# A new hand-made order for attention and two expert layers on one core: other priorities, more filler matmuls, and three edits to the loads

## The chip, the cores and the metric

The kernel runs on 1 core of one Trainium2 chip. Its time is device microseconds (us) of one execution. The kernel before has a median of 481.8 us over 3 runs (479.96 to 482.65).

## The reference

q, k and v have the shape (2, 8, 576, 64): 2 batches, 8 heads, 576 positions of 64 elements. Two attentions are added, and their sum passes through two expert layers (names and checks cut):

```python
q_d, k_d, v_d = (x.reshape(B, H, S // 4, 4, D).mean(axis=3) for x in (q, k, v))
out_up = np.repeat(softmax(scale * q_d @ k_d.T) @ v_d, 4, axis=2)   # 144 positions
mask = abs(pos[:, None] - pos[None, :]) < 4                         # band of 7
out_local = softmax(where(mask, scale * q @ k.T, -1e9)) @ v
x = (out_up + out_local)            # reshaped to 1152 tokens x 512
h = x @ w_in                        # 512 x 2048, float64 in memory
P = a[0] + a[1] * h + a[2] * h**2 + a[3] * h**3
Q = 1.0 + abs(b[0]) * abs(h) + abs(b[1]) * h**2
x = (P / (Q + 1e-06)) @ w_out       # 2048 x 512
h = x @ w_in2
out = (h * tanh(softplus(h))) @ w_out2
```

## The kernel before, in words

The attention is cut into 18 units. A unit is 256 query rows: four windows of 64 positions for a pair of heads, or, for the last 64 positions of a batch, one window for each of the four pairs (the two "mixed" units). For a unit TensorE (PE) transposes the queries (line 552), adds the mask and computes the banded scores (712, 720) and the coarse scores (728), transposes the softmax (797, 802) and multiplies with v (827, 837). In between VectorE (DVE), ScalarE (ACT) and GpSimd (POOL) do the maxima, exponentials, normalisation and copies. Each pair of heads of a batch needs its keys first (lines 552 on PE, 593 on ACT, 603 on DVE). The sum goes as high and low halves into `xh` and `xl`.

The first layer multiplies `xh` and `xl` with `w_in` (line 1155) in three products that give float32 accuracy, applies the rational function, and multiplies with `w_out` (line 1288); its first columns start while attention still runs. The second layer is at lines 1469, 1525 and 1290, with sums of blocks (1329, 1491). Weights come as float64: a load of 1 MB (994, 999), two passes on ACT (1011, 1018), one or two on DVE (1025, 1031), and a split in halves (1037, 1042).

All loads are issued by SyncE (SP) in one queue, with at most 8 under way. The constants `a` and `b` are two small loads from SP (483, 484); ACT takes absolute values of them (515, 516) and DVE derives six numbers (`leading`, 520 to 525).

The order of everything is written out beforehand. Each step is a task with a priority (a due time), engines it may run on with assumed costs, and buffers. `Plan.run` steps through an assumed time and gives every free engine the ready task of the smallest priority. Each engine then executes its instructions in this order and waits on semaphores where data are late. Priorities come from tables: `UOFF` shifts the 18 units, `GOFF` the first weights, `LEAD`, `CLEAD`, `LLEAD`, `OLAG` and `SUMS` whole kinds of tasks.

A filler matmul on zeros (`warm`, line 533, 128x480 in bf16) is counted wherever the assumed time leaves PE idle and a PSUM bank is free. It is emitted only in the window `SHOW`, from 2.4 to 30 us of the assumed time:

```python
if SHOW[0] <= now < SHOW[1]:
    shown = fns[-1](s.view)
```

Of the kernel before, what the change touches and what calls it, by code (L numbers as in the profile page):

```python
# [23 lines left out]
EDGE, LEAST = 2.0 ** -60, 1e-30  # L24


SECOND = 1.8
COLD, FILL_ALL = 3.4, 20
WINDOW, FILL, FILL_END = 3.4, 0.9, 450.0
SHOW = (2.4, 30.0)  # L30
LEAD, CLEAD, LLEAD, OLAG = 38, 14, 40, 18
PROL, PSTEP, VOFF, VROFF, LOFF, KOFF = -45, 2.5, 2, -1, 7, 9
GROUPS = ([6, 6, 4], [4, 4, 4, 4])
KCUT, MIX = 4, (1, 4)
MKP = -45
NKN, NVW, NXT, NQN = 2, 2, 3, 3
XVR, XQN, XVW = 2, 0, 0
SUMS = 5
NRAW, NWT, NRING, NRING2 = 2, 2, 3, (2, 1)
LAT = {"pe": 0.2, "act": 0.16, "dve": 0.15, "pool": 0.15, "sp": 1.1}  # L40
QUEUED = 8
UOFF = [-3.0, 0.0, 0.0, 3.0, 4.5, 3.0, 3.0, -1.5, 6.0, 0.0, 0.0, -4.5, -4.5, 4.5, 6.0, 4.5, -1.5, -1.5]
GOFF = [0.0, 0.0, 0.0, 0.0, -4.0, -4.0, -10.0, -6.0, 2.0, -4.0, 10.0, 12.0]
HP = 15


# [4 lines left out]
def t_dve(n, fast=False, ptr=0):  # L51
    return 0.068 + n * (0.000521 if fast else 0.001042) + 0.06 * ptr
# [28 lines left out]
class Plan:  # L81
# [33 lines left out]
    def run(self, names):  # L115
# [80 lines left out]
        while True:  # L196
            for e in names:
                if until[e] > now:
                    continue
                held = []  # L200
                while ready[e]:
                    item = heapq.heappop(ready[e])
                    t = item[2]
                    if t.started:
                        continue
                    one = next(iter(t.engs))
                    if e != one and until[one] + t.engs[one] <= now + t.engs[e] + SECOND:
# [12 lines left out]
                    end = until[e] = begin + t.engs[e] * (2 if e == "pe" and now < COLD else 1)  # L220
                    there = end + LAT[e]
                    if t.dma:
                        end = begin
                        for issue, move in t.dma:
                            end = max(end, landed[-QUEUED]) + issue
                            moved = max(moved, end + 0.3) + move
                            landed.append(moved + LAT["sp"])
                        until[e], there = end, landed[-1]
                    n += 1
                    heapq.heappush(events, (end, n, 0, e, t))  # L230
                    heapq.heappush(events, (there, n, 1, e, t))
# [43 lines left out]
def kernel(  # L275
# [13 lines left out]
    nc = tc.nc  # L289
    B, H, S, D = q.shape  # L290
# [7 lines left out]
    TW = 384  # L298
# [68 lines left out]
    kn_s = lay("att", NKN, 768, parts=96)  # L367
    vr_s = lay("att", 1, 1024, (4, 4, D), parts=72)
    qn_s = lay("att", NQN, 256)
    vw_s = lay("att", NVW, 512, (4, 2, D), parts=64 + WK)  # L370
    s_s = lay("att", 2, 256, (4, 64))
    pd_s = lay("att", 2, SD)
# [107 lines left out]
        nc.gpsimd.memset(bias1[:, 1:2], 1e-06)  # L480

    def c_sp():
        nc.sync.dma_start(out=a_sb, in_=a.partition_broadcast(128))
        nc.sync.dma_start(out=b_sb, in_=b.partition_broadcast(128))

    add({"act": 1.3}, lambda: nc.scalar.preload_act_table_set("natural_log_exp_and_others"), -1000)
    t_id = add({"pool": 1.1}, lambda: make_identity(nc, ident), -1000)
    t_m = add({"dve": 0.1}, lambda: nc.vector.memset(band, 0.0), -1900)
    t_cd = add({"dve": 0.6}, zeros, -1000)
    add({"dve": 0.4}, lambda: None, -880)  # L490
    t_bn = add({"pool": 0.5}, bands, -900, after=[t_m])
    def mask_set(lo, hi, ws):
        for w in ws:
            masks(*w)
# [2 lines left out]
    t_mk = [  # L497
        add({"dve": cost}, lambda x=x: mask_set(*x), pr, after=[t_bn])
        for cost, pr, x in (
            (0.4, -890, (0, 4, ((0, 0, 1), (0, 1, 1), (0, 2, 1), (0, 3, 1)))), (0.25, MKP, (3, 7, ((1, 4, 4),))),  # L500
            (0.25, MKP, (7, 11, ((2, 8, 4),))),
        )
    ]
    t_bias = add({"pool": 0.1}, biases, -20)
    t_i16 = add({"dve": 0.26}, eyes, -900, after=[t_id])
    t_ab = add({"sp": 0.9}, c_sp, -34, dma=[(0.65, 0.1), (0.5, 0.1)])
    A0, A1, A2, A3 = (cf[:, i:i + 1] for i in range(4))
    S0, S1 = (cf[:, i:i + 1] for i in range(4, 6))

# [16 lines left out]
        tiny(cf[:, 0:3], a_sb[:, 0:3], S0, ALU.mult)  # L526

    t_b = add({"act": 0.25}, absolute, -30, after=[t_ab])
    t_b = add({"dve": 0.6}, leading, -30, after=[t_b])


    def warm(view):
# [21 lines left out]
    def prep(bb, p, prio, slots, start):  # L554
# [58 lines left out]
            dst = vr.v.rearrange("p (h t) f d -> p h (t f d)", h=2)  # L613
            nc.sync.dma_start(out=dst, in_=src)

        m0 = add({"sp": 1.25}, vload, prio + VROFF, take=[vr], chain="vr", dma=[(0.65, 0.8), (0.6, 0.12)])

        def va(e):
            tv = vr.v
# [14 lines left out]
    def unit(u, slots, start):  # L634
# [1 line left out]
        pairs = sorted({p for p, _ in wins})  # L636
        mixed = len(pairs) > 1
        xq, xv = (wide_s["qn"], wide_s["vw"]) if start else ([], [])
        qn, vw, qp, qT, qx = Buf(qn_s + xq), Buf(vw_s + xv), Buf(slots["q"]), Buf(qT_s), Buf(qx_s)
        sc, pt, po, px = Buf(slots["s"]), Buf(slots["pt"]), Buf(slots["po"]), Buf(px_s)  # L640
        tm, s, pd, pT, od, xt = Buf(tm_s), Buf(s_s), Buf(pd_s), Buf(pT_s), Buf(od_s), Buf(xt_s)
        mix = [qx] if mixed else []

        def qload():
            for i, p in enumerate(pairs):
                w, m = wins[i][1], n // len(pairs)
                src = q[bb, 2 * p:2 * p + 2, 64 * w:64 * w + 2 * m, :]
                nc.sync.dma_start(
                    out=qn.v[m * i:m * i + m].rearrange("p (r h d) -> p r h d", h=2, d=D),
                    in_=src.rearrange("h (p r) d -> p r h d", r=2),  # L650
                )

        l0 = add({"sp": 0.65}, qload, prio - LOFF, take=[qn], chain="ld", dma=[(0.65, 0.24)] * 4 if mixed else [(0.65, 0.58)])

        m0 = MASK0[kind]
        keys = [(p, [window(kind, w, b) for b in range(2)]) for p, w in wins]
# [10 lines left out]
                        in_=bass.AP(src.tensor, src.offset + k0 * D, [[D, WK], [far * D, 4], [1, D]]),  # L667
                    )

        vl = add({"sp": 1.0}, vload, prio + VOFF, take=[vw], chain="vw", dma=[(0.45, 0.11)] * 8 if mixed else [(0.45, 0.33)] * 4)  # L670

        def pe_a():
            q2 = qp.v[:, :2 * n].rearrange("c (p r) -> c p r", r=2)
            for r in range(2):
                flip(q2[:, :, r], qn.v, r, n)
# [30 lines left out]
        def pe_b():  # L706
# [24 lines left out]
                        )  # L731

        tb = add(
            {"pe": 1.6 if mixed else 0.86}, pe_b, prio,
            after=tq + [kv_done[p] for p in pairs] + [t_i16, t_mk[kind]],
            take=[sc, tm, s, pd],
            use=[qT] + mix, chain="pb",
# [707 lines left out]
    def seven(st):  # L1445
# [42 lines left out]
        def plus(dst, i, src, after, and_=None):  # L1488
            def fn():
                other = two(dst)[:, i]  # L1490
                nc.vector.tensor_tensor(out=other, in0=src.v[:, :TW], in1=other, op=ALU.add)

            return add({"dve": t_dve(TW)}, fn, pr, after=after, use=[src, dst])

        p1 = prod(A, cols(0, 0), x1[:2], 0, 0, 0, [], [A])
        k1 = copy(low, 0, A, [p1], [low])
# [88 lines left out]
```

## Time and profile before

| | |
|---|---|
| median of 3 runs | 481.8 us |
| profiled execution | 481.31 us |
| its span | 479.5 us |
| PE busy | 467.6 us (98%) |
| DVE, ACT, POOL busy | 376.8, 337.6, 58.7 us |
| granted TensorE clock over the span | 0.993 |

The span leaves 1.8 us of the profiled execution outside. A matmul's row ends when its last column has left the array, so rows of matmuls that follow each other overlap; how densely PE works is read from the starts. Idle time before a row stands in brackets with what ended it. A granted clock of 1.00 is 2.4 GHz, 0.5 is 1.2 GHz.

### The profile page before, as it was taken

The numbers are of one execution on the slowest core, as the hardware profiler recorded it, in microseconds if no ns is written. First come the engines' busy times: TensorE is split into PE (matmuls) and PEld (weight loads), VectorE is DVE, ScalarE is ACT, GpSimd is POOL, SyncE is SP. The second block draws the span as 40 slices with busy tenths as digits, with TensorE's granted clock in tenths as the row PEclk, the third lists the DMA queues.
The fourth block names the chain that finished last, engine by engine and source line by source line (L and its number), as shares of the span: only waits on it lengthen the run. The fifth ranks groups of instructions, "written<-read, shape, count | busy, mean of one in ns | idle before, by whom it ended". The sixth has DMA issues, their size and how long they took to land.

```text
span 479.5 us, 9855 instructions
## 1 busy us (share of the span) xinstructions
PE 467.6 (98%) x4081; PEld 428.5 (89%) x4081; DVE 376.8 (79%) x566; ACT 337.6 (70%) x529; POOL 58.7 (12%) x80
## 2 busy tenths in 40 slices
PE   8999898999999999999999999999999999999996
PEld 4667797889999999999999998898989898989885
DVE  6688789899899978997999989988596669524342
ACT  5778698885988799998878797578667446422320
POOL 2654345653000000000000000000000000000000
PEclk9999799999999999999999999999999999999999
DMA  8967976611422402333022022134314220000103
GB/s 180 234 172 176 263 184 182 153 42 36 168 89 90 143 34 87 106 130 117 0 89 89 1 89 87 45 115 143 137 21 156 87 89 0 1 0 2 66 1 131
DMA packets 45757, 47.17 MB, mean 98 GB/s; under 512 B 30352, under 2 KB 31120, under 8 KB 45712
## 3 DMA queue, kind: packets, MB, share of 16 engines
q1 hardware_dynamic: 45712, 46.54, 33.4%
q8 instruction: 32, 0.52, 0.5%
q14 instruction: 13, 0.11, 0.1%
HBM read 44.17 MB, written 2.36 MB: 97 GB/s over the span
## 4 chain that ended last, share of the span: by engine, by line
PE 74%; DVE 12%; DMA 8%; ACT 3%; issue 1%; SPq 1%; ACTq 0%
PE psum L1290 19%; PE psum L1155 18%; PE psum L1288 15%; PE psum L1469 11%; PE psum L1525 5%; DMA att<-in_q_dram 3%; DMA raw<-in_moe_w_in_dram 3%; PE psum L837 1%; DMA att<-in_v_dram 1%; PE psum L827 1%; DVE wt L1025 1%; PE psum L552 1%; DVE xl L1311 1%; DVE wrk L1329 1%; PE psum L728 1%
## 5 line engine op out<-in xcount | busy, mean ns | idle before, releaser
L1155 PE MATMUL psum<-xh,wi 128*128 128x384 f32 (+1 forms) x336 | 84.7, 323 | 0.2 <-DVE wrk L1184 0.2
L1288 PE MATMUL psum<-gg,wo 128*128 128x384 f32 (+1 forms) x480 | 76.2, 313 | 0.0
L1288 PEld LDWEIGHTS psum<-gg,wo 128*128 128x128 f32 x480 | 72.8, 189 | 0.5 <-issue 0.2
L1155 PEld LDWEIGHTS psum<-xh,wi 128*128 128x128 f32 x336 | 60.2, 193 | 1.5 <-issue 0.9
L1155 PE MATMUL psum<-xl,wi 128*128 128x384 f32 (+1 forms) x168 | 53.1, 316 | 0.0
L1290 PE MATMUL psum<-wo,gg 128*128 128x512 f32 x216 | 51.7, 391 | 0.0
L1290 PE MATMUL psum<-wo,late_g 128*128 128x512 f32 x216 | 51.3, 391 | 0.0
L1290 PEld LDWEIGHTS psum<-wo,late_g 128*128 128x128 f32 x216 | 40.4, 188 | 8.0
L1290 PEld LDWEIGHTS psum<-wo,gg 128*128 128x128 f32 x216 | 40.4, 188 | 8.0
L1025 DVE SCALAR_TENSOR_TENSOR wt<-wt,raw 128x1024 int32<-128x1024 int32 x32 | 40.4, 1266 | 7.5 <-ACT wt L1011 6.5
L1011 ACT ACTIVATE wt<-raw 128x1024 f32<-128x1024 f32 x32 | 36.4, 1137 | 8.7 <-DVE wo L1042 4.8
L1018 ACT ACTIVATE raw<-raw 128x1024 int32<-128x1024 uint16 x32 | 36.8, 1149 | 4.7 <-DMA raw<-in_moe_w_out_dram 3.4
L1525 PE MATMUL psum<-xh,wi 128*128 128x384 f32 x128 | 34.5, 335 | 0.0
L1155 PEld LDWEIGHTS psum<-xl,wi 128*128 128x128 f32 x168 | 32.5, 193 | 0.0
L1401 DVE TENSOR_TENSOR part<-psum,part 128x512 f32<-128x512 f32 x27 | 17.8, 687 | 13.6 <-PE psum L1290 13.6
L1155 PE MATMUL psum<-xh,late_r 128*128 128x384 f32 x96 | 25.5, 334 | 0.0
L1175 ACT ACTIVATE wrk<-psum 128x768 f32<-128x768 f32 (+1 forms) x27 | 19.9, 735 | 6.6 <-PE psum L1155 6.0
L1037 ACT ACTIVATE wo<-wt 128x1024 fp32r<-128x1024 f32 x11 | 11.7, 1061 | 17.7 <-DVE wt L1031 7.7
L1042 DVE TENSOR_TENSOR wo<-wt,wo 128x1024 fp32r<-128x1024 f32 x14 | 17.1, 1218 | 8.7 <-ACT wo L1037 8.7
L1525 PEld LDWEIGHTS psum<-xh,wi 128*128 128x128 f32 x128 | 23.3, 188 | 0.2
L1099 ACT ACT_TABLE_LOAD x17 | 21.8, 1283 | 0.3
L1525 PE MATMUL psum<-xl,wi 128*128 128x384 f32 x64 | 21.4, 335 | 0.0
(164 smaller groups left out, 1038.5 us busy)
## 6 DMA issues: line engine op xcount, KB each, us to landing
raw<-in_moe_w_in_dram SPq DMA_DIRECT2D x16, 1024.0 KB, 5.4
raw<-in_moe_w_out_dram SPq DMA_DIRECT2D x16, 1024.0 KB, 4.9
att<-in_v_dram SPq DMA_DIRECT2D x72, 48.0 KB, 4.0
out_dram<-part SPq DMA_DIRECT2D x9, 256.0 KB, 2.0
att<-in_q_dram SPq DMA_DIRECT2D x16, 128.0 KB, 3.9
att<-in_k_dram SPq DMA_DIRECT2D x6, 288.0 KB, 3.8
att<-in_v_dram SPq DMA_DIRECT2D x6, 288.0 KB
wrk<-in_k_dram SPq DMA_DIRECT2D x2, 288.0 KB, 6.2
```

The source lines that it names most:

```text
L1011: nc.scalar.activation(out=t.v, in_=words(r)[:, :, 1].bitcast(F32), func=AF.Prelu if fold else AF.Identity, scale=2.0 ** -112, **({"alpha" ...
L1018: nc.scalar.activation(out=words(r)[:, :, 0], in_=r.v.bitcast(U16).rearrange("p (n four) -> p n four", four=4)[:, :, 1], func=AF.Copy, sca ...
L1025: nc.vector.scalar_tensor_tensor(out=ti, in0=ti, scalar=3, in1=words(r)[:, :, 0], op0=ALU.logical_shift_left, op1=ALU.bitwise_or)
L1042: ENG[e].tensor_tensor(out=w.v[:, 1], in0=s.v, in1=w.v[:, 0].bitcast(F32), op=ALU.subtract)
L1099: nc.scalar.preload_act_table_set(name)
L1155: nc.tensor.matmul(st.h.v[:, i, :T], w.v[:, ww, ks], xx[:, kk, c0:c0 + T], start=(nn == 0 and (st.big or i == 0)), stop=(nn == 3 * KD - 1 ...
L1175: nc.scalar.activation(out=vw(st.a), in_=H(), func=AF.Square)
L1288: nc.tensor.matmul(A(d)[:, :T], w.v[:, ww, lo + d * 128:lo + (d + 1) * 128], vw(gg)[:, i, :], start=start, stop=stop)
L1290: nc.tensor.matmul(A(d), vw(gg)[:, i, sl], w.v[:, ww, lo:lo + DM], start=start, stop=stop)
L1401: nc.vector.tensor_tensor(out=pv, in0=acc.v[:, j], in1=pv, op=ALU.add)
L1469: nc.tensor.matmul(dst.v[:, :TW], wv.v[:, ww, at:at + 128], x(h, kk), start=bool(take) and nn == 0, stop=nn == 5, skip_group_check=not take,)
L1525: nc.tensor.matmul(h.v[:, i, :TW], w.v[:, ww, at:at + 128], xx[:, kk, c0:c0 + TW], start=nn == 0, stop=nn == 3 * KD - 1)
```

## The change

The tables and constants of the order are new (of `UOFF` and `GOFF` the first lines only). `SHOW` now ends at 450 us, so nearly all counted fillers are emitted. The assumed time of a DMA grows by 0.8 us for every 7.0 us of transfer (`FETCH`). The two loads of constants are issued by ACT, ahead of its first table load; `leading` is computed inside the softmax step of the third unit. A mixed unit loads its queries in one DMA of 64 x 8 x 64 into two neighbouring query buffers and transposes them with four matmuls, instead of four DMAs and two matmuls. The second layer's additions (`plus`) get an earlier due time.

```diff
-SECOND = 1.8
+SECOND = 1.6
-SHOW = (2.4, 30.0)
-LEAD, CLEAD, LLEAD, OLAG = 38, 14, 40, 18
-PROL, PSTEP, VOFF, VROFF, LOFF, KOFF = -45, 2.5, 2, -1, 7, 9
+LEAD, CLEAD, LLEAD, OLAG = 38, 20, 30, 22
+PROL, PSTEP, VOFF, VROFF, LOFF, KOFF = -45, 2.5, 2, 2, 5, 9
-SUMS = 5
+SUMS = 20
-UOFF = [-3.0, 0.0, 0.0, 3.0, 4.5, 3.0, 3.0, -1.5, 6.0, 0.0, 0.0, -4.5, -4.5, 4.5, 6.0, 4.5, -1.5, -1.5]
+FETCH = (0.8, 7.0)
+SHOW = (2.4, 450.0)
+UOFF = [1.5, 0.0, 1.5, 12.0, 13.5, 13.5, 9.0, 18.0, 12.0, 9.0, -3.0, -6.0, -1.5, -3.0, 7.5, 10.5, -1.5, -9.0]
...
-                            moved = max(moved, end + 0.3) + move
+                            first = max(moved, end + 0.3)
+                            moved = first + move + FETCH[0] * (int((first + move) / FETCH[1]) - int(first / FETCH[1]))
...
+    qm_s = [Place("att", qn_s[-2].lo, 512, (8, D), 64)]
...
     def c_sp():
-        nc.sync.dma_start(out=a_sb, in_=a.partition_broadcast(128))
-        nc.sync.dma_start(out=b_sb, in_=b.partition_broadcast(128))
+        nc.scalar.dma_start(out=a_sb, in_=a.partition_broadcast(128))
+        nc.scalar.dma_start(out=b_sb, in_=b.partition_broadcast(128))
...
-    t_ab = add({"sp": 0.9}, c_sp, -34, dma=[(0.65, 0.1), (0.5, 0.1)])
+    t_ab = add({"act": 1.15}, c_sp, -2000, dma=[(0.65, 0.1), (0.5, 0.1)])
...
-    t_b = add({"dve": 0.6}, leading, -30, after=[t_b])
+    t_b = add({"dve": 0.6}, lambda: None, -30, after=[t_b])
...
         def qload():
-            for i, p in enumerate(pairs):
...
+            if mixed:
+                nc.sync.dma_start(out=qn.v, in_=q[bb, :, 64 * w:64 * w + 64].rearrange("h s d -> s h d"))
...
         def pe_a():
+            if mixed:
+                for i in range(nw):
+                    nc.tensor.transpose(
+                        qp.v[:, 64 * i:64 * i + 64], qn.v[:, 2 * i:2 * i + 2].rearrange("s h d -> s (h d)"), ident[:64, :64],
+                    )
+                return
...
             nc.vector.reciprocal(out=tm.v[:, 10:15], in_=tm.v[:, 10:15])
+            if (bb, kind, pairs[0]) == (0, 0, 2):
+                leading()
...
-            return add({"dve": t_dve(TW)}, fn, pr, after=after, use=[src, dst])
+            return add({"dve": t_dve(TW)}, fn, pr - HP, after=after, use=[src, dst])
```

Of instructions, PE has 111 fillers instead of 61, 80 transposes of keys and queries instead of 84 and 8 smaller ones; SP has 10 loads fewer and 2 of a new kind; ACT has the 2 loads of constants and 30 conversions of weights instead of 29, DVE 2 instead of 3 (line 1039). Everything else is the same work in another order.

The first place is ACT's start. Before, in the kernel's own line numbers:

```order
L486 ACT_TABLE_LOAD
L593 ACTIVATE att<-psum 64x288 x4
L682 ACTIVATE att<-psum 128x256
L593 ACTIVATE att<-psum 64x288 x4
L682 ACTIVATE att<-psum 128x256
```

Now (the copies of keys are at line 595):

```order
L486 DMA a_sb<-in_moe_a_dram 128x4
L487 DMA b_sb<-in_moe_b_dram 128x2
L489 ACT_TABLE_LOAD
L517 ACTIVATE b_sb<-b_sb 128x2
L518 ACTIVATE cf<-a_sb 128x4
L595 ACTIVATE att<-psum 64x288 x4
L691 ACTIVATE att<-psum 128x256
```

The two loads and the two absolute values, which need them landed, stand ahead of the first copies of keys.

The second place is SP's queue around the constants and the first mixed unit's queries, before:

```order
L994 DMA raw_75<-in_moe_w_in_dram 128x4x256
L483 DMA a_sb<-in_moe_a_dram 128x4
L484 DMA b_sb<-in_moe_b_dram 128x2
L665 DMA att<-in_v_dram 48x4x64 x8
L994 DMA raw_74<-in_moe_w_in_dram 128x4x256
L648 DMA att<-in_q_dram 32x4x64 x4
L564 DMA att<-in_k_dram 96x12x64
```

And now:

```order
L668 DMA att<-in_v_dram 48x4x64 x8
L651 DMA att<-in_q_dram 128x4x64
L1005 DMA raw_75<-in_moe_w_in_dram 128x4x256
L651 DMA att<-in_q_dram 128x4x64
L668 DMA att<-in_v_dram 48x4x64 x4
L1005 DMA raw_74<-in_moe_w_in_dram 128x4x256
L616 DMA att<-in_v_dram 72x2x512
L668 DMA att<-in_v_dram 48x4x64 x4
L649 DMA att<-in_q_dram 64x8x64
L566 DMA att<-in_k_dram 96x12x64
```

The constants are gone from it, and one load stands for the four of the mixed unit.

The third place is PE at the first mixed unit's product with v, before:

```order
L728 MATMUL psum<-att 32x144 x4
L797 MATMUL psum<-ident,att 112x128 x2
L802 MATMUL psum<-ident,att 72x128 x2
L827 MATMUL psum<-att 64x16 x16
L837 MATMUL psum<-att 64x32 x16
L552 MATMUL psum<-ident,att 128x96 x3
```

And now:

```order
L535 LDWEIGHTS blank
L535 MATMUL psum<-blank 128x480
L808 MATMUL psum<-ident,att 112x128 x2
L813 MATMUL psum<-ident,att 72x128 x2
L535 LDWEIGHTS blank
L535 MATMUL psum<-blank 128x480
L838 MATMUL psum<-att 64x16 x16
L848 MATMUL psum<-att 64x32 x16
L554 MATMUL psum<-ident,att 128x96 x3
```

Fillers (line 535) now stand on both sides of the transposes of the softmax: three ahead, of which the last is shown, and one behind. Over the whole order 71 fillers stand before the first matmul of the first layer (61 before), 39 in the rest of the attention (none before) and 1 later.

## Rows read from the trace of the kernel before

**Rows 1.** The page's busy times: share of the span, instructions.

```profile
PE 467.6 (98%) x4081; PEld 428.5 (89%) x4081; DVE 376.8 (79%) x566; ACT 337.6 (70%) x529; POOL 58.7 (12%) x80
```

**Rows 2.** Stretches: length, busy PE, PEld, DVE, ACT, POOL; clock, DMA share, GB/s.

```profile
0.00:120.00 120.00, 112.89 (x2144) 92.10 (x2144) 101.30 (x244) 91.67 (x227) 57.98 (x79) 0.97 0.68 162
120.00:260.00 140.00, 140.00 (x846) 140.00 (x844) 127.36 (x140) 123.61 (x144) 0.75 (x1) 1.00 0.28 98
```

**Rows 3.** PE in order of time, fillers: start, duration, line [idle before].

```profile
9.42 1.58 PE L533 MATMUL psum<-blank 128*128 128x480 bf16 x7
10.84 0.41 PE L552 MATMUL psum<-ident,wrk 96*128 96x96 f32 x3
```

**Rows 4.** PE in order of time, waits before 31 us.

```profile
7.34 0.69 PE L552 MATMUL psum<-ident,att 96*128 96x96 f32 x6 [0.47 <-DMA att<-in_k_dram]
9.14 0.44 PE L552 MATMUL psum<-ident,att 128*128 128x128 f32 x2 [0.34 <-DMA att<-in_q_dram]
```

**Rows 5.** PE in order of time, waits from 31 to 120 us.

```profile
35.60 0.28 PE L1155 MATMUL psum<-xl,wi 128*128 128x256 f32 x1
35.72 0.28 PE L1155 MATMUL psum<-xh,wi 128*128 128x256 f32 x1
36.41 0.45 PE L827 MATMUL psum<-att 72*64 72x64 f32 x8 [0.42 <-DVE att L857]
...
39.94 0.41 PE L552 MATMUL psum<-ident,att 128*128 128x128 f32 x2 [0.51 <-DMA att<-in_q_dram]
...
50.71 0.30 PE L837 MATMUL psum<-att 48*64 48x32 f32 x2
52.51 1.03 PE L837 MATMUL psum<-att 48*64 48x32 f32 x30 [1.50 <-DMA att<-in_v_dram]
...
76.57 0.69 PE L552 MATMUL psum<-ident,att 96*128 96x96 f32 x5 [1.13 <-ACT att L593]
77.99 0.40 PE L797 MATMUL psum<-ident,att 128*112 128x128 f32 x2 [0.72 <-POOL att L786]
...
99.69 0.38 PE L1155 MATMUL psum<-xh,wi 128*128 128x256 f32 x1 [0.20 <-DVE wrk L1184]
```

**Rows 6.** Stretches around the lower clock, columns as in Rows 2.

```profile
52.00:56.00 4.00, 3.49 (x63) 3.21 (x67) 2.39 (x4) 1.98 (x5) 1.83 (x4) 0.57 1.03 377
56.00:60.00 4.00, 4.00 (x49) 3.50 (x42) 2.76 (x6) 1.77 (x6) 0.38 (x1) 0.57 0.97 127
```

**Rows 7.** PE's waits: total us, times, longest.

```profile
PE psum L1469 <- DVE wrk L1491: 0.9, 1, 0.9
```

**Rows 8.** SP's queue in order of time: start, duration until issued.

```profile
23.74 1.65 SPq L483 DMA_DIRECT2D a_sb<-in_moe_a_dram  x1
25.43 1.17 SPq L484 DMA_DIRECT2D b_sb<-in_moe_b_dram  x1
26.65 6.19 SPq L665 DMA_DIRECT2D att<-in_v_dram  x8
...
33.38 2.62 SPq L648 DMA_DIRECT2D att<-in_q_dram  x4
```

**Rows 9.** The page's DMA issues: count, KB each, median us to landing.

```profile
out_dram<-part SPq DMA_DIRECT2D x9, 256.0 KB, 2.0
...
att<-in_k_dram SPq DMA_DIRECT2D x6, 288.0 KB, 3.8
...
a_sb<-in_moe_a_dram SPq DMA_DIRECT2D x1, 2.0 KB, 8.0
b_sb<-in_moe_b_dram SPq DMA_DIRECT2D x1, 1.0 KB, 6.5
```

**Rows 10.** ACT in order of time, its start and the absolute values.

```profile
0.73 1.28 ACT L486 ACT_TABLE_LOAD   x1 [0.73 <-PEq L1569]
5.00 1.75 ACT L593 ACTIVATE att<-psum 64x288 f32<-64x288 f32 x4 [2.99 <-PE psum L552]
...
32.56 0.19 ACT L515 ACTIVATE b_sb<-b_sb 128x2 f32<-128x2 f32 x1
```

**Rows 11.** DVE in order of time, first and last of seven instructions of `leading`.

```profile
32.87 0.16 DVE L520 TENSOR_REDUCE cf<-cf 128x1 f32<-128x4 f32 x1 [0.73 <-ACT cf L516]
...
33.90 0.23 DVE L512 TENSOR_SCALAR cf<-a_sb,cf 128x3 f32<-128x3 f32 x1
```

More of the change, by code (lines that the diff above doesn't have):

```diff
@@ L41 @@
 QUEUED = 8
-UOFF = [-3.0, 0.0, 0.0, 3.0, 4.5, 3.0, 3.0, -1.5, 6.0, 0.0, 0.0, -4.5, -4.5, 4.5, 6.0, 4.5, -1.5, -1.5]
-GOFF = [0.0, 0.0, 0.0, 0.0, -4.0, -4.0, -10.0, -6.0, 2.0, -4.0, 10.0, 12.0]
+FETCH = (0.8, 7.0)
+SHOW = (2.4, 450.0)
+UOFF = [1.5, 0.0, 1.5, 12.0, 13.5, 13.5, 9.0, 18.0, 12.0, 9.0, -3.0, -6.0, -1.5, -3.0, 7.5, 10.5, -1.5, -9.0]
+GOFF = [0.0, 2.0, 0.0, 2.0, -4.0, -4.0, -4.0, -20.0, 18.0, 0.0, -6.0, 22.0]
 HP = 15
@@ L489 @@
     t_cd = add({"dve": 0.6}, zeros, -1000)
-    add({"dve": 0.4}, lambda: None, -880)
-    t_bn = add({"pool": 0.5}, bands, -900, after=[t_m])
+    t_bn = add({"pool": 1.0}, bands, -900, after=[t_m])
     def mask_set(lo, hi, ws):
@@ L499 @@
         for cost, pr, x in (
-            (0.4, -890, (0, 4, ((0, 0, 1), (0, 1, 1), (0, 2, 1), (0, 3, 1)))), (0.25, MKP, (3, 7, ((1, 4, 4),))),
-            (0.25, MKP, (7, 11, ((2, 8, 4),))),
+            (0.8, -890, (0, 4, ((0, 0, 1), (0, 1, 1), (0, 2, 1), (0, 3, 1)))), (0.5, MKP, (3, 7, ((1, 4, 4),))),
+            (0.5, MKP, (7, 11, ((2, 8, 4),))),
         )
@@ L614, in vload @@
             nc.sync.dma_start(out=dst, in_=src)
-        m0 = add({"sp": 1.25}, vload, prio + VROFF, take=[vr], chain="vr", dma=[(0.65, 0.8), (0.6, 0.12)])
+        m0 = add({"sp": 0.65}, vload, prio + VROFF, take=[vr], chain="vr", dma=[(0.65, 1.0)])
         def va(e):
@@ L638, in unit @@
         xq, xv = (wide_s["qn"], wide_s["vw"]) if start else ([], [])
-        qn, vw, qp, qT, qx = Buf(qn_s + xq), Buf(vw_s + xv), Buf(slots["q"]), Buf(qT_s), Buf(qx_s)
+        qn, vw, qp, qT, qx = Buf(qm_s if mixed else qn_s + xq), Buf(vw_s + xv), Buf(slots["q"]), Buf(qT_s), Buf(qx_s)
         sc, pt, po, px = Buf(slots["s"]), Buf(slots["pt"]), Buf(slots["po"]), Buf(px_s)
@@ L644, in qload @@
         def qload():
-            for i, p in enumerate(pairs):
-                w, m = wins[i][1], n // len(pairs)
-                src = q[bb, 2 * p:2 * p + 2, 64 * w:64 * w + 2 * m, :]
+            w = wins[0][1]
+            if mixed:
+                nc.sync.dma_start(out=qn.v, in_=q[bb, :, 64 * w:64 * w + 64].rearrange("h s d -> s h d"))
+            else:
                 nc.sync.dma_start(
-                    out=qn.v[m * i:m * i + m].rearrange("p (r h d) -> p r h d", h=2, d=D),
-                    in_=src.rearrange("h (p r) d -> p r h d", r=2),
+                    out=qn.v.rearrange("p (r h d) -> p r h d", h=2, d=D),
+                    in_=q[bb, 2 * pairs[0]:2 * pairs[0] + 2, 64 * w:64 * w + 2 * n].rearrange("h (p r) d -> p r h d", r=2),
                 )
-        l0 = add({"sp": 0.65}, qload, prio - LOFF, take=[qn], chain="ld", dma=[(0.65, 0.24)] * 4 if mixed else [(0.65, 0.58)])
+        l0 = add({"sp": 0.65}, qload, prio - LOFF, take=[qn], chain="ld", dma=[(0.45 if mixed else 0.65, 0.58)])
         m0 = MASK0[kind]
@@ L668, in vload @@
                     )
-        vl = add({"sp": 1.0}, vload, prio + VOFF, take=[vw], chain="vw", dma=[(0.45, 0.11)] * 8 if mixed else [(0.45, 0.33)] * 4)
+        vl = add({"sp": 1.0}, vload, prio + VOFF, take=[vw], chain="vw", dma=[(0.45, 0.33)] * 4)
         def pe_a():
+            if mixed:
[4 more added lines that the diff above has]
+                return
             q2 = qp.v[:, :2 * n].rearrange("c (p r) -> c p r", r=2)
@@ L733, in unit @@
         tb = add(
-            {"pe": 1.6 if mixed else 0.86}, pe_b, prio,
+            {"pe": 1.52 if mixed else 0.78}, pe_b, prio,
             after=tq + [kv_done[p] for p in pairs] + [t_i16, t_mk[kind]],
```

## The prediction

> **What bounds the kernel now.** I read the page's busy times first, then the stretches, then TensorE's (PE's) own order of time. The reader is to see that PE is busy 98% of the span, the next engine 79% [rows 1], and that PE shows no idle time at all from 120 to 260 us, at a granted clock of 1.00 [rows 2]. All it loses lies in the attention stage: 120.00 − 112.89 = 7.1 us idle there [rows 2], and what it does with fillers. So the accounting is made on PE's queue alone. PE executes in its written order, and its own work (scores, transposes, products of both layers) is the same before and after in count and shape but for the mixed units' few transposes. Hence time after = time before + fillers added − waits that go + waits that come.
>
> The waits that could go are these. Before 31 us there are two, for keys and for queries, shown as 0.47 + 0.34 us [rows 4]. From 31 to 120 us there are eight, five of them 0.42 + 0.51 + 1.50 + 1.13 + 0.72 = 4.3 us and three smaller ones of 0.7 us together [rows 5]: 5.0 us. With the two before and 1.2 us ahead of the first instruction this makes the 7.1 us. Each wait is longer than shown, because a matmul's row runs on after the next could have started: the matmul at 35.72 followed its forerunner by 0.12 us, so the next could start at 35.84 and did at 36.41, 0.57 us lost for 0.42 shown; at 50.71, where two matmuls stand, 52.51 − 50.71 less some 0.04 for the two is 1.76 for 1.50 shown [rows 5]. I add 0.2 us to each: 1.2 us early, 6.6 us from 31 to 120. One more stands in the second layer, 0.9 us shown, 1.1 with the addition [rows 7]. And after the wait of 1.50 us the granted clock shows 0.57 in both stretches of 4 us from 52 to 60 [rows 6]: with 1.0 and 0.5 as the two levels, (1 − 0.57) / 0.5 = 86% of 8 us, 6.9 us, at 1.2 GHz, in which half the work was lost, 3.4 us. All that can go: 1.2 + 6.6 + 1.1 + 3.4 = 12.3 us.
>
> **The change part by part.** *Fillers.* 50 more, 111 instead of 61. Seven of them took 10.84 − 9.42 = 1.42 us, 0.203 each [rows 3], so PE's queue gets 50 × 0.203 = 10.1 us longer. A filler is executed whether or not PE would have waited there; it is free only if it stands in a wait. Ten come before the first matmul of the first layer, where just 1.2 us of waits are left beside the 61 that stand there already: at most one tenth of that stretch can be hidden. 39 come in the rest of the attention, 7.9 us against 6.6 us of waits.
>
> *The order.* It may take away up to the 12.3 us. What it leaves I bound by none and by as much as now. Between them the nearest row is the stretch that already has fillers at the places where the order foresees waits: from 4 to 31 us PE waited 1.2 us [rows 4], 0.045 us per us. At that rate 89 us leave 4.0 us. I take this: the new order, like the one before in its early part, foresees most but not all. The wait in the second layer sits at the additions whose due time is moved forward; I count it as gone, and the lower clock too, since it followed the one long wait in a stretch without fillers.
>
> *The clock, by the notes.* The granted clock fell once, after 1.5 us of waiting, and stayed at 1.00 from 60 us on with no filler at all [rows 2, 6]. The Trainium skill ("TensorE: Matmul & The Clock Gate", HAM oscillation) says in essence that gaps in PE's work bring the half clock back and that a kernel should be arranged to keep PE busy. By that rule fillers are worth having; here the trace prices what they can save at the 3.4 us already in the sum, against 10.1 us that they cost.
>
> *Constants over ScalarE (ACT).* SP is relieved of 1.65 + 1.17 = 2.8 us of issuing, but the eight loads of v behind needed 6.19 us for what is usually about 0.5 each, so SP waited for buffers there anyway [rows 8]; nothing is counted. The cost is at ACT's start. Its first copies of keys began at 5.00 us after 2.99 us idle [rows 10]. Now two issues (2.8 us from about 0.73), the table load of 1.28 us and two absolute values of 0.19 stand ahead, and the latter wait for the landing. The second issue begins at 0.73 + 1.65 = 2.4. With the landing of the fastest row, 2.0 us, nothing changes, as the table load ends at 4.8; with its own 6.5 us it lands at 8.9 and the copies start at 9.1, 4.1 us late [rows 9, 10]. I take the 3.8 us of the loads of keys, which also start in an empty queue: landing at 6.2, copies at 6.4, 1.4 us late. Behind them PE waits for the first unit's keys, and what is left of the two early waits vanishes in this one: 1.4 us in all before 31 us.
>
> The 8.0 and 6.5 us to landing were measured behind a 1 MB load of weights in the same queue [rows 8, 9]. The Trainium skill ("DMA: Bandwidth & Descriptors", Queues, rings and completion order) says that a DMA engine takes turns between the queues it has work for, packet by packet, so the small loads would not stand behind SP's; no run here shows a second queue in use. By that rule the late end of 4.1 us is unlikely, and the sum would lose at most the 1.4.
>
> *`leading`.* Seven small DVE instructions from 32.87 to 34.13, 1.3 us [rows 11], move to the third unit, where their inputs are long there. DVE is 84% busy in the stage (101.30 of 120) [rows 2]; they are not on PE's queue and cost nothing, 1.3 us on that unit's softmax if uncovered, or as much back at the old place.
>
> *Mixed queries.* One issue instead of four saves SP some 2.62 × 3/4 = 2.0 us at 33 us [rows 8]; the wait at 39.94 for queries, 0.51 us, and the one at 52.51 for v stand behind it [rows 5] and are already in the 12.3. It takes two query buffers at once, so the next query load may be held until both are free. PE's four smaller transposes replace two; no row has their size, and between nothing and the 0.41 us of three transposes [rows 3] I take nothing.
>
> The sum on the profiled execution: 479.5 + 10.1 − 12.3 + 4.0 + 1.4 = 482.7 us of span; with the 1.8 us outside 484.5. The median shown is 0.5 us above the profiled execution, so **485.0 us** against 481.8, 0.7% slower.
>
> **The rivals.** First, *fillers fall into waits one for one*: the 39 later ones sit just where PE would have waited, and almost no wait is left beside them, 0.8 instead of 4.0. Then 485.0 − 3.2 = 481.8, no change, not slower. For it: the 7.9 us of fillers there and the 6.6 + 3.4 us lost now are of one size. Against it: one kind of wait comes from ACT, one from POOL, two from DMA [rows 5], and an order must foresee all. It decides if fewer than about 1.7 us of waits stay from 31 to 120 us.
>
> Second, *ACT's first copies wait for the constants in full*: 4.1 us instead of 1.4, 485.0 + 2.7 = 487.7. It decides if the constants land after some 8 us. For it their own 8.0 and 6.5 us, against it the empty queue.
>
> Third, *the new order foresees no better than the old*: fillers are added and the 12.3 us stay, 485.0 + 12.3 − 5.4 = 491.9. For it: nothing in the trace says that assumed transfer times were the cause of the waits for ACT and POOL, 1.9 of the 4.3 us. Against it: the clock need not fall again.
>
> Fourth, *faster*: if no wait is left anywhere, 485.0 − 5.4 = 479.6 us, 0.5% below. That is the floor of this accounting, so a clear gain needs PE to work more densely than its rows show now.
>
> **How the numbers follow.** Changes within 0.5% (479.4 to 484.2) can't be told from none. My forecast has 0.45, with its own range from 482.5 to 487.5, of which about 0.38 lies above 484.2 and 0.07 below; one for one 0.33; the constants 0.07; no better foresight 0.08 (488 to 492); faster 0.07. So slower is 0.38 + 0.07 + 0.08 = 0.53, no change 0.07 + 0.33 = 0.40, faster 0.07. The range that leaves two in ten out reaches from the floor, 479.5, to 491.
>
> **What would show it.** In the profile after, PE's fillers must number 111 and take about 0.2 us each; the eight waits from 31 to 120 us should shrink to about 4 us; the granted clock should read 1.00 from 52 to 60; the first copies of keys should start near 6.4 us; from 120 us on PE should be as dense as before, reaching the same matmul some 3 us later. I am wrong on the faster side if waits vanish and PE's groups run denser than now; on the slower side if a new long wait, with a lower clock behind it, stands where the loads were moved.

## The result: 0.8% slower

The changed kernel took 483.27 us (median of 22 runs), the kernel before 480.1 us beside it (22 runs): a ratio of 1.0078, 95% interval 1.0058 to 1.0097, so slower by more than 0.5%. The profiled execution has a span of 481.7 us against 479.5. The forecast of 485.0 against 481.8 was a ratio of 1.0066.

The page's busy times after, answering [rows 1], and the group of the fillers (busy us, mean ns of one, idle before):

```profile
PE 474.3 (98%) x4135; PEld 430.6 (89%) x4135; DVE 379.9 (79%) x565; ACT 339.8 (71%) x530; POOL 56.9 (12%) x80
...
L535 PE MATMUL psum<-blank 128*128 128x480 bf16 x111 | 28.0, 381 | 1.2 <-DVE band L491 1.2
```

PE is busy 6.7 us longer and has 54 more instructions, 50 of them fillers. The stretches after, columns as in [rows 2], answering [rows 2, 6]:

```profile
0.00:120.00 120.00, 116.83 (x2129) 92.35 (x2130) 103.08 (x243) 93.46 (x226) 54.54 (x78) 1.00 0.67 161
120.00:260.00 140.00, 140.00 (x900) 139.80 (x900) 127.04 (x139) 121.87 (x144) 2.40 (x3) 1.00 0.30 98
31.00:120.00 89.00, 88.28 (x1672) 75.42 (x1671) 80.94 (x170) 74.07 (x174) 39.81 (x51) 1.00 0.63 157
52.00:56.00 4.00, 4.00 (x68) 3.73 (x67) 3.93 (x11) 2.84 (x10) 1.52 (x4) 1.00 1.13 307
56.00:60.00 4.00, 4.00 (x72) 3.64 (x71) 3.75 (x8) 3.79 (x7) 1.12 (x1) 1.00 0.85 203
```

PE is idle 3.2 us up to 120 us where it was 7.1, and 0.7 us from 31 us on; the clock stands at 1.00 throughout. By its busy share PE looks better everywhere, and the kernel is slower: the added busy time is fillers. What PE still waits for (total us, times, longest), answering [rows 5, 7]:

```profile
PE psum L535 <- DVE band L491: 1.2, 1, 1.2
PE psum L554 <- DMA att<-in_k_dram: 0.8, 1, 0.8
PE psum L554 <- ACT att L691: 0.6, 1, 0.6
PE psum L1480 <- DVE wrk L1502: 0.5, 1, 0.5
```

Where the time was lost is read from one matmul that both kernels have: the first one of the first layer with a weight that lies in the attention's freed space. PE in order of time, before:

```profile
106.97 0.26 PE L712 MATMUL psum<-mask,eye 64*32 64x192 bf16 x4
...
146.18 0.33 PE L1155 MATMUL psum<-xh,late_r 128*128 128x384 f32 x1
```

And after:

```profile
111.24 0.26 PE L721 MATMUL psum<-mask,eye 64*32 64x192 bf16 x4
...
148.34 0.33 PE L1166 MATMUL psum<-xh,late_r 128*128 128x384 f32 x1
```

The first row of each is the scores of the last unit: 4.3 us later. The second, which I call the mark below, comes 2.2 us later, as much as the spans differ; from it to the end it is 333.3 us before and 333.4 after. In this pair all of the loss stands ahead of the mark. The profiled execution of before, 479.5 us at a mean clock of 0.993, is one of its longer ones: 62 others, timed beside the experiments, have spans from 473.8 to 480.2 us. So the 2.2 us are less than the 3.2 us between the medians.

### The profile page after: what moved, and what is told of

It is laid out like the page before. It is cut to its first block, busy times and chain, and to the rows that moved or that the text cites. A ratio compares the mean times of both kernels' runs of the same rounds, so it can differ in the third digit from the quotient of the medians.

```text
span 481.7 us, 9964 instructions
## 1 busy us (share of the span) xinstructions
PE 474.3 (98%) x4135; PEld 430.6 (89%) x4135; DVE 379.9 (79%) x565; ACT 339.8 (71%) x530; POOL 56.9 (12%) x80
## 4 chain that ended last, share of the span: by engine, by line
PE 78%; DVE 12%; ACT 6%; DMA 2%; issue 1%; POOL 0%; ACTq 0%; SPq 0%
PE psum L1301 18%; PE psum L1166 17%; PE psum L1299 13%; PE psum L1480 11%; PE psum L1536 5%; PE psum L535 4%; PE psum L848 2%; PE psum L554 1%; PE psum L838 1%; PE psum L729 1%; DVE wt L1036 1%; PE psum L737 1%; DMA raw<-in_moe_w_in_dram 1%; DVE part L1389 1%; PE psum L808 1%
## 5 line engine op out<-in xcount | busy, mean ns | idle before, releaser
L1166 PEld LDWEIGHTS psum<-xh,wi 128*128 128x128 f32 x336 | 59.1, 189 | 1.7 <-issue 1.1
L1036 DVE SCALAR_TENSOR_TENSOR wt<-wt,raw 128x1024 int32<-128x1024 int32 x32 | 39.4, 1231 | 6.4 <-ACT wt L1022 3.6
L535 PE MATMUL psum<-blank 128*128 128x480 bf16 x111 | 28.0, 381 | 1.2 <-DVE band L491 1.2
L1536 PEld LDWEIGHTS psum<-xh,wi 128*128 128x128 f32 x128 | 23.3, 188 | 0.2
```

The lines of the kernel that those rows point to most:

```text
L535: nc.tensor.matmul(view[:, :480], blank[:, :128], blank, start=True, stop=True)
L1036: nc.vector.scalar_tensor_tensor(out=ti, in0=ti, scalar=3, in1=words(r)[:, :, 0], op0=ALU.logical_shift_left, op1=ALU.bitwise_or)
L1166: nc.tensor.matmul(st.h.v[:, i, :T], w.v[:, ww, ks], xx[:, kk, c0:c0 + T], start=(nn == 0 and (st.big or i == 0)), stop=(nn == 3 * KD - 1 ...
L1536: nc.tensor.matmul(h.v[:, i, :TW], w.v[:, ww, at:at + 128], xx[:, kk, c0:c0 + TW], start=nn == 0, stop=nn == 3 * KD - 1)
```

## The experiments

Twelve kernels, in three groups (e1 to e4, e5 to e8, e9 to e12), each group timed beside its own runs of before, whose medians are 479.4, 479.1 and 478.5 us. The ratio is to these; the mark and the span are those of the profiled execution, in us.

| run | order | fillers | mark | span | ratio, 95% interval |
|---|---|---|---|---|---|
| before | before | 61 | 146.18 | 479.5 | 1 |
| after | after | 111 | 148.34 | 481.7 | 1.0078 (1.0058 to 1.0097) |
| e1 | after | 71 | 150.56 | 484.0 | 1.0158 (1.0132 to 1.0185) |
| e2 | before | 80 | 143.47 | 477.0 | 0.9987 (0.9965 to 1.0010) |
| e3 | after | 3 | 151.09 | 484.5 | 1.0169 (1.0132 to 1.0207) |
| e4 | before | 3 | 142.20 | 475.5 | 0.9959 (0.9943 to 0.9975) |
| e5 | before, three edits | 61 | 142.14 | 475.4 | 1.0000 (0.9967 to 1.0034) |
| e6 | before, three edits | 3 | 143.62 | 476.9 | 0.9967 (0.9946 to 0.9988) |
| e7 | after, second weight early | 105 | 148.18 | 481.3 | 1.0102 (1.0074 to 1.0130) |
| e8 | planned again | 100 | 147.76 | 482.5 | 1.0088 (1.0065 to 1.0112) |
| e9 | planned again | 60 | 146.56 | 486.4 | 1.0199 (1.0160 to 1.0238) |
| e10 | planned again | 106 | 148.47 | 486.0 | 1.0172 (1.0141 to 1.0203) |
| e11 | planned again | 92 | 145.85 | 478.9 | 1.0052 (1.0030 to 1.0074) |
| e12 | planned again | 89 | 148.80 | 482.8 | 1.0097 (1.0063 to 1.0131) |

### Do the fillers cost it? (e1 to e4)

Theory A is the prediction's: a filler is 0.2 us on PE's queue. Theory B: the fillers stand in waits. Only the stretch in which fillers are put into the program changes, the order stays:

```diff
-SHOW = (2.4, 450.0)      # after
+SHOW = (2.4, 30.0)       # e1
+SHOW = (2.4, 3.5)        # e3
-SHOW = (2.4, 30.0)       # before
+SHOW = (2.4, 450.0)      # e2
+SHOW = (2.4, 3.5)        # e4
```

> The changed kernel with the filler window ended at 30 us again (SHOW = 2.4 to 30.0): the same order on every engine, 71 fillers instead of 111, none after the first matmul of the first layer. Theory A (a filler costs PE its 0.2 us except where PE would have waited, and only part of the 39 late ones stands in waits): 40 x 0.203 = 8.1 us less, of which about half comes back as waits, and perhaps one fall of the clock: ratio to the kernel before 0.995 to 1.004, faster than the changed kernel. Theory B (the fillers stand in waits and are free; the new order itself is slower): as the changed kernel, 1.006 to 1.010, with 6 to 8 us of waits shown from 31 to 120 us where it showed 0.7.

> The kernel before with the filler window opened to 450 us (SHOW = 2.4 to 450.0): the same order, 80 fillers instead of 61. Theory A: 19 x 0.203 = 3.9 us more on PE, less the waits and the clock that they cover: ratio 1.000 to 1.006, granted clock 1.00 throughout if the one long wait is all that lowers it. Theory B: fillers are free and keep the clock up: 0.993 to 1.000.

> The changed kernel with fillers in the first 3.5 us of the assumed time alone (3 instead of 111), the same order. Theory A: what stands before the first layer's first matmul waits for loads and weights whatever fills the time, so the 68 early fillers return as waits almost in full, 0 to 3 us gained there beside the gain of e1; but the clock may stay at its lower level through the first 30 us and slow the early matmuls. Ratio 0.990 to 1.005. Theory B: 1.006 to 1.015, the clock lower in several places.

> The kernel before with fillers in the first 3.5 us of the assumed time alone (3 instead of 61), the same order. Theory A: PE waits where the fillers stood, since the first layer's first matmul comes when its weights are converted at about 30 us; time as before or up to 2 us less, unless the clock falls in the gaps: 0.995 to 1.003. Theory B: slower by the low clock in the first 40 us, 1.003 to 1.015.

For the late fillers theory A fell, and theory B was too low: the ratios of e1 and e3 lie above its ranges as well. Without the 40 later fillers, 8.1 us of PE's queue, the changed kernel became 0.8% slower still. What PE waits for in e1 from 31 to 120 us (total us, times, longest):

```profile
PE psum L554 <- ACT att L691: 1.8, 2, 1.0
PE psum L1299 <- DVE gg L1265: 1.4, 1, 1.4
PE psum L808 <- POOL att L792: 1.2, 1, 1.2
PE psum L721 <- ACT att L768: 0.9, 1, 0.9
PE psum L729 <- ACT att L691: 0.4, 1, 0.4
```

That is 5.7 us where after shows 0.7, with 8.1 us of fillers. The fillers do not fit the waits exactly. At 40 us eleven of them stand in after ahead of two transposes, which start at 42.34 (rows under e7). These need POOL's row, which in after ended at 40.99; in e1 they wait for POOL and start at 42.37:

```profile
40.48 0.51 POOL L792 TENSOR_TENSOR att<-att 128x192 f32<-128x192 f32 x1 [2.87 <-DVE att L785]
```

```profile
42.37 0.43 PE L808 MATMUL psum<-ident,att 128*112 128x128 f32 x2 [1.18 <-POOL att L792]
```

The profiled execution of e1 ran 1.3 us late ahead of this wait (the seventh unit's scores at 37.35 instead of 36.03), late from its start on, and the fillers of after outlast the wait by as much. The stretches of e1, columns as in [rows 2]:

```profile
40.00:50.00 10.00, 8.47 (x150) 6.74 (x149) 7.86 (x14) 8.63 (x21) 4.09 (x4) 0.83 0.91 177
90.00:100.00 10.00, 7.03 (x112) 6.15 (x112) 8.07 (x20) 6.46 (x18) 3.98 (x6) 0.83 0.35 109
```

PE waits 1.5 and 3.0 us in stretches where after shows it busy with fillers, and behind these waits the granted clock falls: 0.83 in each stretch, between the levels of 1.2 and 2.4 GHz. The Trainium skill ("TensorE: Matmul & The Clock Gate", HAM oscillation) says that waits between PE's pieces of work send it back to the half clock; e1 agrees, with 0.83 where after shows 1.00.

So the late fillers stand mostly in waits, and they hold the clock up. What they may still cost can be bounded. Had all the time at the half clock cost half, the median span of e1, 485.7 us at a mean clock of 0.989, would be 480.4 us at the full one. This estimate is 1.1 us below after at a full clock (481.5) and 3.9 us above before at a full clock (476.5; both figures are explained further down). So at most about 1.1 of the 8.1 us is a cost, and the new order is slower without its late fillers too.

In the order of before the same edit does nothing that can be told (e2), and leaving out 58 of the early fillers gains 0.4% (e4), though the clock falls to 0.83 there as well. Here theory A held, with 0.995 to 1.003, and theory B fell. The stretch of e4:

```profile
20.00:40.00 20.00, 15.92 (x369) 12.26 (x370) 16.27 (x43) 14.98 (x39) 10.79 (x14) 0.83 0.87 213
```

PE waits 4.1 us of these 20. That slow work between such waits costs little is my reading; no run holds the clock up there. With 3 fillers the new order is again the slower one, 1.0169 against 0.9959, but part of that is the clock, whose mean over a run is 0.924 to 0.985 in e3 and 0.989 to 0.993 in e4.

### Do the three edits beside the order cost it? (e5, e6)

The order of before is held instruction for instruction and only the constants, `leading` and the mixed units' loads are changed, the latter into a tile of their own:

```diff
-nc.sync.dma_start(out=a_sb, ...); nc.sync.dma_start(out=b_sb, ...)       # behind the second weight
+nc.scalar.dma_start(out=a_sb, ...); nc.scalar.dma_start(out=b_sb, ...)   # first on ACT; absolute() before the first copies
+            if (bb, kind, pairs[0]) == (0, 0, 2):
+                leading()
+nc.sync.dma_start(out=mixed_q, in_=q[bb, :, 64 * w:64 * w + 64].rearrange("h s d -> s h d"))
-SHOW = (2.4, 30.0)       # e6 only
+SHOW = (2.4, 3.5)
```

> The kernel before with its order held instruction for instruction and its 61 fillers; only the three edits beside the order are made: the constants loaded over ScalarE's queue at its start (and their absolute values taken there), `leading` in the third unit's softmax, and one load with four transposes for each of the two mixed units (into a tile of its own, so that no query buffer is held). Theory O (the loss sits in the order): 0.996 to 1.001 of before. Theory E (the edits cost it: the first key copies 0.3 us late, the four transposes 0.4 us twice, `leading` 2.7 us on VectorE instead of 1.3): 1.003 to 1.008, with the same waits as after.

> As e5_before_three_edits, with 3 fillers instead of 61 (those from 2.4 to 3.5 us), as in e4_before_first_fillers, which measured 0.996. Theory O: 0.992 to 0.997, the edits take nothing from it. Theory E: 1.000 to 1.005.

The edits show no cost: 1.0000 in e5 (0.9967 to 1.0034) and 0.9967 in e6, both inside theory O. ACT's start in e5 has the same shape as after (start, us, engine, line):

```profile
0.73 0.42 ACTq L492 DMA_DIRECT2D a_sb<-in_moe_a_dram  x1
1.18 0.47 ACTq L493 DMA_DIRECT2D b_sb<-in_moe_b_dram  x1
1.68 1.28 ACT L495 ACT_TABLE_LOAD   x1 [1.68 <-PEq L1591]
4.77 0.20 ACT L524 ACTIVATE b_sb<-b_sb 128x2 f32<-128x2 f32 x1 [1.81 <-DMA b_sb<-in_moe_b_dram]
4.88 0.19 ACT L525 ACTIVATE cf<-a_sb 128x4 f32<-128x4 f32 x1
5.27 1.75 ACT L602 ACTIVATE att<-psum 64x288 f32<-64x288 f32 x4 [0.20 <-PE psum L561]
```

The copies start at 5.27 instead of 5.00 [rows 10], and ACT waits for PE, not for the constants. With e4 and e6 two versions stand 0.3 to 0.4% below before; the edits add nothing to e4 that can be told. Two things are not tested: in after the mixed load holds two query buffers, here it has a tile of its own; and the edits were not taken out of the new order. For the first, no wait of e1 from 31 to 120 us was ended by a load.

### Is it the late second weight? (e7)

The longest unbroken row of late fillers in after's trace stands at 40 us. (Fifteen more stand in three groups from 88.97 to 93 us; no run moves what is around those.) PE in order of time:

```profile
39.90 0.38 PE L813 MATMUL psum<-ident,att 128*72 128x128 f32 x2
40.12 2.39 PE L535 MATMUL psum<-blank 128*128 128x480 bf16 x11
42.34 0.38 PE L808 MATMUL psum<-ident,att 128*112 128x128 f32 x2
...
43.90 0.46 PE L1166 MATMUL psum<-xh,wi 128*128 128x256 f32 x1
...
49.40 0.26 PE L721 MATMUL psum<-mask,eye 64*32 64x192 bf16 x4
```

Eleven fillers, 2.2 us, and the row at 43.90 is the first with the second weight. On SP's queue its load now stands behind eight loads of v that wait for buffers, and is issued at 28.25:

```profile
19.33 8.16 SPq L668 DMA_DIRECT2D att<-in_v_dram  x8
27.58 0.61 SPq L651 DMA_DIRECT2D att<-in_q_dram  x1
28.25 0.63 SPq L1005 DMA_DIRECT2D raw<-in_moe_w_in_dram  x1
```

The experiment holds the order of after and moves ten pieces by hand (in the plan's time, from and to):

```diff
+load 26.65 -> 18.0 (between the two units' loads of v)
+scale 33.73 -> 31.0   low 35.29 -> 33.8    (ACT)
+join 36.49 -> 34.85   lo 40.02 -> 37.7     (DVE)   hi 38.66 -> 36.3 (ACT)
+four pieces of the first layer 41.34 -> 39.5 (PE), six fillers ahead of them left out
```

> The changed kernel with its order held, but for the first layer's second weight: its load goes ahead of the last four of the eight v loads that wait for buffers, its five conversions move 3 to 5 us forward on ScalarE and VectorE into idle time, and the first twelve matmuls with it take the place of six of the eleven fillers at 40 us. Theory W (the late weights are the loss of the new order): the 2.4 us that PE spends on fillers at 40 us come back, 1.003 to 1.0045 of before where after has 1.008. Rival S (the loss is spread over the order, and the next wait takes the place of this one): 1.006 to 1.009. In the trace the first matmuls with the second weight should start near 41 us instead of 43.9 either way.

(In the plan's time the five conversions moved 1.5 to 2.7 us, not 3 to 5.) PE in order of time in e7:

```profile
40.28 1.18 PE L543 MATMUL psum<-blank 128*128 128x480 bf16 x5
41.12 0.46 PE L1174 MATMUL psum<-xh,wi 128*128 128x256 f32 x1
...
42.22 0.51 PE L1174 MATMUL psum<-xh,wi 128*128 128x256 f32 x2 [0.52 <-DVE wi L1061]
...
48.42 0.78 PE L543 MATMUL psum<-blank 128*128 128x480 bf16 x3
49.14 0.26 PE L729 MATMUL psum<-mask,eye 64*32 64x192 bf16 x4
```

The edit did what it says: the second weight is used 2.8 us earlier. But its matmuls now stand in front of the eighth unit's scores, which came at 44.25 instead of 43.08, and wait 0.52 us for a conversion on DVE. The ninth unit's scores came at 49.14 instead of 49.40, the mark 0.16 us earlier, and the ratio 1.0102 is not below after's. Theory W fell; rival S is right in kind: 1.0102 lies above its 1.006 to 1.009, and the interval, from 1.0074, reaches into it. What PE waits for at 40 us without fillers e1 shows: POOL's part of a unit's softmax, and not the weight.

### Is it the new numbers, or the counting of packets? (e8 to e12)

The order comes from a planner in the kernel, which places each task by its own clock; every one of these kernels is planned again. The end of the last task by that clock, no measurement, is 471.2 for before and 475.6 for after. The plan of after also assumes other costs, in lines that the diff above leaves out: bands and masks cost twice as much, the loads of v and the banded scores have new figures. No run varies these alone.

```diff
 # e8: after with before's UOFF, GOFF, LEAD..., PROL..., SUMS, SECOND and
+FETCH = (0, 7.0)
 # e9: before with one number changed
-GOFF = [0.0, 0.0, 0.0, 0.0, -4.0, ...]
+GOFF = [0.0, 2, 0.0, 0.0, -4.0, ...]
 # e10: after with
+FETCH = (0, 7.0)
 # e11: e10 with 11 numbers tuned for the shortest plan; e12: e8 with 7, likewise
```

> The changed kernel, edits and late fillers included, planned again with the numbers of before (offsets of units and weights, leads, sums) and with packets not counted (0 us instead of 0.8 per 7 us of transfer). Theory O in its narrow form (the new numbers are the worse ones): 0.996 to 1.002. Rival R (the numbers of before suit only the order of before; whatever else the plan reckons with moves instructions everywhere and loses as much): 1.005 to 1.015.

> The kernel before, planned again with one number changed: the second weight's offset is 2 instead of 0, nothing else. The plan's own clock, by which it places the instructions, puts the end of its last task at 471.2 for before, 475.7 for after and 476.6 for e8_after_old_numbers; here at 480.9. Theory P (the loss is the plan's: the new order is a longer one already by the plan's own reckoning, and the chip follows that with some 0.8 us per us, as 1.0078 and 1.0088 did): 479.5 + 0.8 x 9.7 us, 1.013 to 1.02. Rival Q (the plan's reckoning says little; orders near each other run alike): 0.998 to 1.005.

> The changed kernel with its numbers, planned again with packets not counted (0 us instead of 0.8 per 7 us of transfer). The plan's own end is 479.5. Theory P: 479.5 + 0.8 x 8.3 us, 1.010 to 1.017. Rival F (counting packets is what lengthens the order): under 1.005.

> The changed kernel with packets not counted and the numbers tuned further from its own for the shortest plan (thirteen of them changed); edits and late fillers as in after. The plan's own end is 472.4. Theory P: 479.5 + 0.8 x 1.2 us, 0.999 to 1.005. Rival Q: as after and e8, 1.006 to 1.011.

> As e11_after_retuned, but tuned from the numbers of before (seven of them changed). The plan's own end is 472.4 too. Theory P: 0.999 to 1.005. Rival Q: 1.006 to 1.011, as e8_after_old_numbers, which it starts from.

(In e11 eleven numbers were changed beside the packets, not thirteen.)

| | e11 | e12 | after | e8 | e10 | e9 |
|---|---|---|---|---|---|---|
| plan's end, less before's (us) | 1.2 | 1.2 | 4.5 | 5.4 | 8.3 | 9.7 |
| measured: (ratio - 1) x 479.5 (us) | 2.5 | 4.7 | 3.7 | 4.2 | 8.2 | 9.5 |

With the old numbers and no packets the loss is the same (e8, as rival R had it), with the new numbers and no packets twice as large (e10, so rival F fell), and a single offset in before costs 2% (e9). So neither the numbers nor the counting is the cause by itself. That numbers are good only for the exact plan that they were tuned in is my reading of these five. Theory P, that the loss was there in the plan's own reckoning, held for e9, was missed by 0.0002 in e10 and in e11, and failed for e12, which lost 4.7 us for 1.2 as rival Q had it. For after itself the plan reckons 4.5 us more and 3.7 were measured. In e9 nearly all of the loss stands behind the mark, in e10 part of it: from the mark to the end of the span it is 339.8 and 337.5 us instead of 333.3. The largest wait of e9 there, PE in order of time:

```profile
289.18 5.99 PE L1288 MATMUL psum<-gg,wo 128*128 128x384 f32 x24 [3.25 <-DVE part L1378]
```

With one offset of an early weight changed, a wait of 3.25 us stands in front of the first layer's last products with `w_out`, 143 us behind the mark.

## Why the prediction was right in size and wrong in its reason

- **Fillers, +10.1 us.** This step failed. 111 fillers stand there at 0.203 us, as predicted (seven from 5.59 to 7.01 us), and PE's queue is 10.1 us longer; but the late ones are not the cost: without them e1 is slower, and at most about 1.1 of their 8.1 us is a cost. The ten early ones were not tested alone. I set the 39 late fillers against the waits of the old order, 6.6 us, and called the rest a loss. They stand mostly in waits of the new order, which [rows 5] cannot show.
- **Waits and clock, -12.3 us, of which 4.0 come back.** The clock read 1.00 from 52 to 60 us, as forecast. From 31 to 120 us 0.7 us of idle time is left instead of 4.0, in the second layer 0.5 of 0.9. But the new order has waits of the same size, with fillers in them: without its late fillers e1 shows 5.7 us there, and before showed 5.0. How much the new order adds shows where the clock hardly fell: in the 17 of 62 runs of before (beside the experiments) with a mean clock of 0.999 or more the median span is 476.5 us, in 16 of the 22 of after 481.5. That is 5.0 us, of which the steadier clock gives back some on average: before's mean clock is 0.996, after's 0.999. The 5.0 is rough, since the two come from different rounds: beside after, before's median was 0.7 to 1.6 us longer than beside the experiments.
- **The sum.** It gave 482.7 of span against 481.7 measured, but single terms were off by more and in part cancelled, so the near hit is in part luck. In idle time shown, the waits from 31 to 120 us fell by 4.3 us (5.0 to 0.7) where the sum had 2.6 (6.6 less 4.0). Those in the second layer fell by 0.4 where it had 1.1, and those before 31 us rose by 0.3 (2.1 to 2.4) where it had 0.2 (1.4 less 1.2). An account of PE's queue adds up whatever the cause, because a wait and a filler in its place are one length; it says how long, not why.
- **Constants.** The copies came 0.3 us late, not 1.4. Two issues took 0.41 + 0.47 us at the start of an empty queue, not the 1.65 + 1.17 of [rows 8], and the absolute values could start 3.9 us after the second issue began, near the 3.8 us to landing of the key loads [rows 9] that I took. So a second queue is shown at an empty start; beside a 1 MB load no run shows it. The start after:

```profile
0.73 0.41 ACTq L486 DMA_DIRECT2D a_sb<-in_moe_a_dram  x1
1.18 0.47 ACTq L487 DMA_DIRECT2D b_sb<-in_moe_b_dram  x1
1.67 1.28 ACT L489 ACT_TABLE_LOAD   x1 [1.67 <-PEq L1580]
5.06 0.20 ACT L517 ACTIVATE b_sb<-b_sb 128x2 f32<-128x2 f32 x1 [2.10 <-DMA b_sb<-in_moe_b_dram]
...
5.32 1.74 ACT L595 ACTIVATE att<-psum 64x288 f32<-64x288 f32 x4
```

- **`leading` and the mixed units.** No cost that can be told, as said, by e5; `leading` itself took 2.9 us instead of 1.3 [rows 11], and the four small transposes 0.39 us (47.12 to 47.51) where I took nothing and bounded by 0.41.
- **The same matmul some 3 us later.** It is 2.2 us later at the mark, and dense from there on.
- **The rivals.** The first (fillers one for one into waits) describes what the late fillers do. Its sign came, less than 1.7 us of waits from 31 to 120 us, and of the forecast's own signs two failed: about 4 us of waits there, and the copies near 6.4 us (5.32). But its time did not come, 481.8, no change: like the forecast it missed that the waits are new. The second (constants in full) did not come: 0.3 us for 4.1. The third (no better foresight) blamed the order too, but for waits that stay, and 0.7 us of 5.0 stayed.

What in the order makes those waits is open. The late second weight alone is not it (e7), and none of e1's waits from 31 to 120 us was ended by a load: ACT, DVE and POOL end them. Where the loss lies, a comparison with e5 shows, which has the same edits, the order of before, and in its profiled execution a clock of 1.00 as well:

```profile
31.00:120.00 89.00, 86.22 (x1728) 76.99 (x1728) 80.21 (x170) 74.73 (x179) 43.86 (x51) 1.00 0.65 162
```

PE is idle 2.8 us there and has at most three fillers, 0.6 us. In after, idle time and the 39 fillers come to 0.7 + 7.9 = 8.6 us. So some 5 of the 6.2 us between the two marks (148.34 and 142.14) arise from 31 to 120 us. The scores of the ninth, twelfth, fifteenth and last unit come 4.1, 6.0, 3.5 and 8.3 us later than in e5, but the new offsets move units on purpose, so such a distance is no loss by itself.

## What to carry to other kernels

When a new schedule brings its own fillers, compare the time of one matmul that both kernels must reach, not busy shares: fillers make a slower order look denser. Take the fillers out of the new order before you blame them, and read the clock when you do; put the small edits into the old order held still. Here one run each (e1, e5) said most about both. And expect a change of the plan's inputs to cost something by itself: the five orders planned again here lost 0.5 to 2%, one of them by a single offset.

## What the runs showed of the hardware

A one-column DVE instruction took 1.1 us. DVE in order of time in after, the first five of the seven of `leading`:

```profile
18.48 0.12 DVE L522 TENSOR_REDUCE cf<-cf 128x1 f32<-128x4 f32 x1
18.63 0.15 DVE L514 TENSOR_SCALAR cf<-cf 128x1 f32<-128x1 f32 x1
18.82 1.10 DVE L524 TENSOR_TENSOR cf<-cf 128x1 f32<-128x1 f32 x1
19.84 0.14 DVE L514 TENSOR_SCALAR cf<-a_sb 128x1 f32<-128x1 f32 x1
20.02 0.75 DVE L526 SCALAR_TENSOR_TENSOR cf<-cf 128x1 f32<-128x1 f32 x1
```

And POOL beside it:

```profile
18.63 1.27 POOL L622 TENSOR_TENSOR wrk<-wrk 72x512 f32<-72x512 f32 x1 [1.21 <-DMA wrk<-in_v_dram]
19.98 0.72 POOL L626 TENSOR_TENSOR att<-wrk 72x256 f32<-72x256 f32 x1
```

The DVE row of 1.10 us ends at 19.92, POOL's at 19.90; that of 0.75 ends at 20.77, POOL's at 20.70. The TENSOR_SCALAR of 0.14 falls between POOL's two instructions, and the one at 18.63, beside POOL's first, took 0.15. In before POOL had nothing to do at this place. The row of DVE, and POOL's first row behind it:

```profile
33.25 0.16 DVE L522 TENSOR_TENSOR cf<-cf 128x1 f32<-128x1 f32 x1
34.99 1.31 POOL L781 TENSOR_TENSOR att<-att 128x192 f32<-128x192 f32 x1 [3.15 <-ACT att L682]
```

The same instruction took 0.16 us there, and all seven 1.3 us. In e8 it took 1.02 us and ended at 20.78, as did a POOL instruction (20.39 and 0.39 long), and the SCALAR_TENSOR_TENSOR behind it, with POOL idle, took 0.16. So in these traces two kinds of DVE instruction lasted until a POOL instruction beside them ended. In after that is 0.94 + 0.59 us of the 1.6 us by which `leading` grew.
